# A one-row attention and MLP mix: the output weights streamed as the moving operand, the result kept as a row, other score shares, and b2 on another queue

## The chip, the cores and the metric

The kernel runs on one core of one Trainium2 chip. The metric is the device time in microseconds; shown are the median of three runs and the one execution that the profiler recorded. A core has TensorE (PE), VectorE (DVE), ScalarE (ACT), GpSimd (POOL) and SyncE (SP), each with its own instruction stream. They wait for each other by semaphores. DMAs are issued from an engine's stream; nearly all of this kernel's come from SyncE.

## The reference

One token goes through two branches, and a gate mixes them:

```python
g = sigmoid((x * gate_w).sum(-1, keepdims=True))
q = (x @ wq) as 32 heads of 128;  k, v: caches of 32 heads x 4096 x 128, bf16
o = softmax(q k^T * 128**-0.5) v            # per head, one query row
a = o.reshape(1, 1, 4096) @ wo              # wo: 4096 x 512
b = relu(x @ w1 + b1)**2 @ w2 + b2          # 512 -> 1376 -> 512
return g * a + (1 - g) * b                  # 512 values
```

The caches are 67.1 MB together, the four weight matrices some 11.2 MB. Each is read once.

## The kernel before

**Tiles.** Four heads make one tile, so there are eight tiles (`NQ`). A partition holds 128 consecutive positions of one head (32 partitions per head, `NB` = 128 "blocks" of 128 values). A K tile and a V tile are 4 MB each. K tiles go round three buffers `Kt`, V tiles round two buffers `Vt`; the last two V tiles go into `Kt` (`VT`). The weights wq lie in `Vt` slot 1, wo in `Vt` slot 0, and w1 and w2 in `Kt` slot 2, where K tile 2 (the third) goes later.

**Scores in three shares.** Of the 128 blocks of a tile, 4 times 17 (`GP`, `GB`) are multiplied on GpSimd (L301) and summed on VectorE (`psums`, L662). Two times 14 (`XP`, `XH`) are multiplied and summed on VectorE (`prods` L649, `sums` L657). The last 32 are transposed on TensorE (L424) in four pieces of eight, copied by ScalarE (L330), multiplied by q on TensorE (`scores`, L438) and copied beside the others (`score_copy`, L336). VectorE takes the maximum (L669), TensorE and VectorE bring it to one value per head (`max_rows` L448, L673, `max_cols` L452), ScalarE takes the exponentials (L347). `pv` (L469) multiplies them with V in four column groups of TensorE; `pv_copy` (L353) and `extract` (L478) collect each head's row in `O`.

**Order of the loads.** SyncE issues wq, K0, w1, w2 in three pieces, eight small pieces of w2 (L272, behind a wait for a memset of their place), K1 and V0. `load_k(2)` waits for the MLP's last matmul (`s_ml`, set after L528), since the MLP weights lie in its slot. Then the V and K tiles alternate, each behind a wait for its buffer, then wo in five pieces (L283) and the output (L286). The small vectors x, gate_w, b1 and b2 are issued by ScalarE (L308 to L311).

**Order at the start.** TensorE turns x into columns, then transposes b2 (L393), projects q in eight groups of four matmuls (L409), with a transpose of each finished group between them (`q_columns`, L400), and goes on to tile 0 (transposes, scores), the MLP's hidden row (L499, L502), its columns (L510), and the second matrix (L528). VectorE computes the gate (L620 to L624), then b2 times 1 - g (`b2g`, L627), then copies the odd groups of q (`qb`, L637), then starts on the tiles. ScalarE copies the even groups (L322). `q_columns` of a group waits for its copy, and a projection into a PSUM tile `T` waits for the copy of the group three before.

**End.** After the last `extract`, VectorE divides (L711), `regroup` (L540) and a copy (L713) put the attention row into 128 partitions x 32 columns, `o2`. `attn_out` (L549) runs through the 32 row groups of wo: per group four matmuls with a 128 x 128 piece of wo as the weights and one column of o2 as the moving operand. They add into `acc`, four columns that already hold the MLP's output (`mlp_cols`, L534). VectorE adds b2g (L716), TensorE transposes to four rows (L593), VectorE copies (L718), SyncE stores.

Of the kernel before, what the change touches and what calls it, by code (L numbers as in the profile page):

```python
# [5 lines left out]
def bass_gated_mix__gqa_block_cached__dense_activation_squared_relu__decode_kernel(  # L6
# [43 lines left out]
    GB = 17  # L50
    XP = 2
    XH = 14
    XB = GP * GB + XP * XH
    YB = NB - XB
    TC = 8
    NC = YB // TC
# [8 lines left out]
    BIG = 3.0e38  # L65
    TS = [0, 8, 16, 24, 30, 32]
    NW = len(TS) - 1

# [10 lines left out]
    with ctx:  # L79
# [18 lines left out]
        pr = sb("pr", [128, XH, 128], fp32)  # L98
        pg = sb("pg", [128, 2, GB, 128], fp32)
# [12 lines left out]
        b2r = sb("b2r", [4, 128], bf16)  # L112
# [4 lines left out]
        fin4 = sb("fin4", [4, 128], bf16)  # L117
# [23 lines left out]
        b2g = sb("b2g", [128, 4], fp32)  # L141
        fin = sb("fin", [128, 4], bf16)

        T = [pb(f"T{i}", [128, 512], fp32) for i in range(NT)]
# [11 lines left out]
        B2 = pS[:, 400:402].bitcast(bf16)  # L156
        H = pX[:, 160:160 + FN + TX]
        HX = pX[:, 224:224 + TX]
        acc = pX[:, 256:260]
# [8 lines left out]
        S = pS[:, 0:4 * YB].rearrange("p (b h) -> p b h", h=4)  # L168
# [7 lines left out]
        s_b2 = sem("s_b2")  # L176
        s_oc = sem("s_oc")
        s_o2 = sem("s_o2")
        s_fT = sem("s_fT")
        s_f4 = sem("s_f4")  # L180
# [42 lines left out]
        s_mc = sem("s_mc")  # L223
        s_hv = sem("s_hv")
# [6 lines left out]
        with nc.Block() as block:  # L231

            @block.sync
            def _(eng):
                def load_k(i):
                    if i >= NK:
                        eng.wait_ge(s_t, NC * (i - NK + 1))
                        eng.wait_ge(s_mu, XP * (i - NK + 1))
                        eng.wait_ge(s_pm, GP * (i - NK + 1))
                    if i == 2:  # L240
                        eng.wait_ge(s_ml, 1)
                    eng.dma_start(Kt[:, i % NK, :], k_p[i * 128:(i + 1) * 128, :]).then_inc(s_k[i % NK], 16)

                def load_v(i):
                    if i == 1:
                        eng.wait_ge(s_qr, NQ)
                        eng.wait_ge(s_h, 2)
                    if i < NQ - 2:
                        if i >= NV:
                            eng.wait_ge(s_pv, i - NV + 1)  # L250
                        eng.dma_start(VT(i), v_p[i * 128:(i + 1) * 128, :]).then_inc(s_v[i % NV], 16)
                        return
                    eng.wait_ge(s_t, NC * i)
                    eng.wait_ge(s_mu, XP * i)
                    eng.wait_ge(s_pm, GP * i)
                    if i == NQ - 2:
                        eng.dma_start(VT(i), v_p[i * 128:(i + 1) * 128, :]).then_inc(s_vl[0], 16)
                    else:
                        for u in range(2):
                            eng.dma_start(VT(i)[:, u * 8192:(u + 1) * 8192],  # L260
                                          v_p[i * 128:(i + 1) * 128, u * 8192:(u + 1) * 8192])\
                               .then_inc(s_vl[1 + u], 16)
# [6 lines left out]
                eng.wait_ge(s_wm, 1)  # L269
# [15 lines left out]
                eng.wait_ge(s_f4, 1)  # L285
                eng.dma_start(out[0, 0, :].rearrange("(j p) -> j p", p=128), fin4[:, :]).then_inc(s_out, 16)  # L286

            @block.gpsimd
            def _(eng):
# [4 lines left out]
                for i in range(NQ):  # L294
                    eng.wait_ge(s_k[i % NK], 16 * (i // NK + 1))
                    eng.wait_ge(s_qd if i % 2 else s_qb, 4 * (i // 2 + 1))
                    for k in range(GP):
                        n = GP * i + k
                        if n >= 2:
                            eng.wait_ge(s_ps, n - 1)  # L300
                        eng.tensor_tensor(pg[:, n % 2, :, :], Kt[:, i % NK, k * GB * 128:(k + 1) * GB * 128]  # L301
                                          .rearrange("p (b d) -> p b d", b=GB),
                                          qb[:, i:i + 1, :].broadcast_to([128, GB, 128]), ALU.mult)\
                           .then_inc(s_pm, 1)

            @block.scalar
            def _(eng):
# [3 lines left out]
                eng.dma_start(b2r[:, :], B_b2.rearrange("(j p) -> j p", p=128)).then_inc(s_b, 16)  # L311
# [20 lines left out]
                def score_copy(i):  # L332
                    eng.wait_ge(s_sc, NC * (i + 1))
                    for h in range(4):
                        a, b = HP * h, HP * h + HP
                        eng.activation(Sb[a:b, i % NS, XB:NB], S[a:b, :, h], ACT.Copy).then_inc(s_cp, 1)  # L336
# [18 lines left out]
                for i in range(NQ + 1):  # L355
                    if i == NQ:
                        pv_copy(NQ - 3)
                        pv_copy(NQ - 2)
                    if i < NQ:
                        for c in range(NC):  # L360
                            evac(i * NC + c)
                            if c == 1 and i >= 3:
                                pv_copy(i - 3)
                        score_copy(i)
                        if i == 0:
                            eng.wait_ge(s_h, 1)
                            for u, a in enumerate(range(0, F, 512)):
                                b = min(a + 512, F)
                                eng.activation(hrow[:, a:b], T[u][0:1, 0:b - a], ACT.Copy).then_inc(s_hw, 1)
# [4 lines left out]
                    if i >= 1:  # L374
                        neg_max(i - 1)
                        exps(i - 1)
                pv_copy(NQ - 1)

            @block.tensor
            def _(eng):  # L380
# [11 lines left out]
                eng.wait_ge(s_b, 32)  # L392
                eng.transpose(B2, b2r[:, :], ident[0:4, 0:4]).then_inc(s_b2, 1)  # L393
# [22 lines left out]
                def transposes(n):  # L416
                    i, c = n // NC, n % NC
# [4 lines left out]
                    for y in range(TC):  # L422
                        w = XB + c * TC + y
# [4 lines left out]
                def scores(n):  # L428
                    i, c = n // NC, n % NC
# [26 lines left out]
                def pv(i, a, b):  # L456
# [8 lines left out]
                    if a == NG // 2 and i == NQ - 1:  # L465
# [29 lines left out]
                def mlp_h():  # L495
                    eng.wait_ge(s_w1, 16)
                    parts = [(u, a, min(a + 512, F)) for u, a in enumerate(range(0, F, 512))]
# [8 lines left out]
                def mlp_c():  # L506
                    eng.wait_ge(s_hw, 3)
# [23 lines left out]
                def mlp_cols():  # L531
                    eng.wait_ge(s_mc, 1)
                    for j in range(4):
                        eng.matmul(acc[:, j:j + 1], pvf[0:112, j * 128:j * 128 + 128], pick[0:112, 0, 28:29],  # L534
                                   start=(j == 0), stop=False, skip_group_check=True)
# [9 lines left out]
                def attn_out(c):  # L545
                    eng.wait_ge(s_wo[c], 16)
                    for t in range(TS[c], TS[c + 1]):
                        for j in range(4):
                            mm = eng.matmul(acc[:, j:j + 1], wo_sb[:, t, j * 128:(j + 1) * 128],  # L549
                                            o2[:, t:t + 1], start=False, stop=(t == 31),  # L550
                                            skip_group_check=True)
                    if c == NW - 1:
                        mm.then_inc(s_acc, 1)

                for i in range(NQ):
                    for c in range(NC):
                        transposes(i * NC + c)
                        if c >= 2:
                            scores(i * NC + c - 2)
                    scores(i * NC + NC - 2)  # L560
                    scores(i * NC + NC - 1)
# [15 lines left out]
                    if i >= 2:  # L577
                        pv(i - 2, NG // 2, NG)
                extract(NQ - 3)
                pv(NQ - 2, 0, NG // 2)  # L580
                pv(NQ - 2, NG // 2, NG)
                max_rows(NQ - 1)
                max_cols(NQ - 1)
                extract(NQ - 2)
                den()
                pv(NQ - 1, 0, NG // 2)
                pv(NQ - 1, NG // 2, NG)
                extract(NQ - 1)
                regroup()
                for c in range(NW):  # L590
                    attn_out(c)
                eng.wait_ge(s_fin, 1)
                eng.transpose(T[2][0:4, 0:64].bitcast(bf16), fin[:, :], ident[:, :]).then_inc(s_fT, 1)  # L593

            @block.vector
            def _(eng):
                eng.memset(WX, 0.0).then_inc(s_wm, 1)
# [28 lines left out]
                eng.wait_ge(s_b2, 1)  # L626
                eng.tensor_scalar(b2g[:, :], B2, omg[:, 0:1], None, ALU.mult)\  # L627
# [13 lines left out]
                def prods(i, u):  # L641
# [4 lines left out]
                    if n >= 1:  # L646
                        eng.wait_ge(s_sd, n)
                    a = GP * GB + u * XH
                    eng.tensor_tensor(pr[:, :, :], Kt[:, i % NK, a * 128:(a + XH) * 128]  # L649
                                      .rearrange("p (b d) -> p b d", b=XH),  # L650
                                      PQ[:, i % 4:i % 4 + 1, :].broadcast_to([128, XH, 128]), ALU.mult)\
                       .then_inc(s_mu, 1)

                def sums(i, u):
                    eng.wait_ge(s_mu, XP * i + u + 1)
                    a = GP * GB + u * XH
                    eng.tensor_reduce(Sb[:, i % NS, a:a + XH], pr[:, :, :], AX.X, ALU.add).then_inc(s_sd, 1)  # L657

                def psums(i, k):
                    n = GP * i + k  # L660
                    eng.wait_ge(s_pm, n + 1)
                    eng.tensor_reduce(Sb[:, i % NS, k * GB:(k + 1) * GB], pg[:, n % 2, :, :], AX.X, ALU.add)\  # L662
# [53 lines left out]
                eng.tensor_tensor(fin[:, :], acc[:, 0:4], b2g[:, :], ALU.add).then_inc(s_fin, 1)  # L716
                eng.wait_ge(s_fT, 1)
                eng.tensor_copy(fin4[:, :], T[2][0:4, 0:64].bitcast(bf16)).then_inc(s_f4, 1)  # L718
# [29 lines left out]
```

## Time and profile before

| | |
|---|---|
| median of three runs | 190.68 us (190.45 to 191.6) |
| the profiled execution | 191.37 us, of which the span from first to last instruction is 189.9 us |
| DVE busy | 154.5 us, 81% of the span |
| POOL busy | 137.8 us, 73% |
| PE busy | 108.5 us, 57% |
| ACT busy | 69.4 us, 37% |
| moved by DMA | 78.47 MB, 413 GB/s over the span |

Times in the profile's timeline count from the start of the span. A row there gives start and length in us, engine, line, operation, what is written from what, and in brackets the idle time ahead of it and what ended it. In the list of groups a row gives total busy time and the mean of one instruction in ns. In the list of waits a row gives total us, number and the longest. DMA rows end with the us from issue to landing.

### The profile page before, as it was taken

What the parts mean: (1) busy time and instruction counts of PE and PEld (TensorE: products, weight loads), DVE (VectorE), ACT (ScalarE), POOL (GpSimd) and SP (SyncE); (2) the same over time, 40 slices, a digit from 0 to 9 for tenths busy, and PEclk for the clock granted to TensorE, in tenths of its full rate; (3) what the DMA queues carried; (4) which work ended last, traced back from release to release, by engine and by line L of the source; (5) the groups of instructions that cost most, each with busy time, mean ns of one, the idle gap of its engine ahead of it and who ended that gap; (6) DMA issues with size and microseconds to landing.
All of it is one profiled execution on the core that took longest, in us unless ns stands there. A gap on an engine that the chain in (4) does not pass through costs nothing. (4 is left out here: it accounts for less than half of the span.)

```text
span 189.9 us, 2665 instructions
## 1 busy us (share of the span) xinstructions
PE 108.5 (57%) x1092; PEld 67.4 (35%) x1092; DVE 154.5 (81%) x134; ACT 69.4 (37%) x170; POOL 137.8 (73%) x38
## 2 busy tenths in 40 slices
PE   1129867658213549408922881468076818685866
PEld 0113243318213516405712461327041814343245
DVE  6112479799999999999999999999999999994010
ACT  2103455208151807800960294049105730613210
POOL 1000299948799899989998999899989989970000
PEclk9999999556755855855575575586755555566555
DMA  6999999999999999999999999999999999999990
GB/s 221 443 442 442 399 470 404 428 421 421 440 437 435 428 442 438 435 414 421 421 431 442 435 435 425 421 442 442 425 421 421 435 442 442 390 425 418 419 389 30
DMA packets 3840, 78.47 MB, mean 413 GB/s; under 512 B 483, under 2 KB 589, under 8 KB 886
## 3 DMA queue, kind: packets, MB, share of 16 engines
q1 hardware_dynamic: 3816, 78.32, 96.7%
q8 instruction: 8, 0.13, 0.3%
q14 instruction: 2, 0.02, 0.0%
q10 hardware_dynamic: 14, 0.01, 0.0%
HBM read 78.32 MB, written 0.00 MB: 412 GB/s over the span
## 5 line engine op out<-in xcount | busy, mean ns | idle before, releaser
L301 POOL TENSOR_TENSOR pg<-Kt,qb 128x2176 f32<-128x2176 bf16 x32 | 137.1, 4316 | 31.1 <-DMA Kt<-in_A_k_cache_dram 21.1
L662 DVE TENSOR_REDUCE Sb<-pg 128x17 f32<-128x2176 f32 x32 | 76.9, 2404 | 0.0
L330 ACT ACTIVATE kT<-T 128x1024 bf16<-128x1024 bf16 x32 | 30.8, 1030 | 7.0 <-PE T L424 6.7
L649 DVE TENSOR_TENSOR pr<-Kt,pQ 128x1792 f32<-128x1792 bf16 x16 | 32.2, 2011 | 1.0
L657 DVE TENSOR_REDUCE Sb<-pr 128x14 f32<-128x1792 f32 x16 | 32.0, 2003 | 0.0
L424 PE MATMUL T<-ident,Kt 128*128 128x128 bf16 x256 | 26.2, 285 | 8.3 <-DMA Kt<-in_A_k_cache_dram 8.3
L424 PEld LDWEIGHTS T<-ident,Kt 128*128 128x128 bf16 x256 | 22.9, 133 | 12.8 <-DMA Kt<-in_A_k_cache_dram 9.8
L469 PE MATMUL pO<-Vt,E 128*16 128x512 bf16 x192 | 25.1, 604 | 0.0
L340 ACT ACTIVATE nM<-pM 128x4 f32<-128x4 f32 x8 | 1.4, 173 | 62.0 <-PE pM L452 62.0
L448 PE MATMUL pM<-identf,mp 128*1 128x128 f32 x8 | 2.9, 360 | 31.2 <-DVE mp L669 31.2
L347 ACT ACTIVATE E<-Sb,nM 32x128 bf16<-32x128 f32 x32 | 18.8, 586 | 1.0
L438 PE MATMUL pS<-qc,kT 128*128 128x4 bf16 x256 | 11.7, 168 | 9.3 <-ACT kT L330 9.0
L478 PE MATMUL pX<-pvf,pick 112*32 112x128 f32 x64 | 15.3, 421 | 2.3 <-ACT pvf L353 2.3
L438 PEld LDWEIGHTS pS<-qc,kT 128*128 128x128 bf16 x256 | 9.9, 102 | 11.4 <-ACT kT L330 11.3
L478 PEld LDWEIGHTS pX<-pvf,pick 112*32 112x32 f32 x64 | 9.9, 168 | 7.0 <-ACT pvf L353 4.1
L448 PEld LDWEIGHTS pM<-identf,mp 128*1 128x1 f32 x8 | 0.6, 80 | 32.3 <-DVE mp L669 32.3
L637 DVE CAST qb<-T 32x128 bf16<-32x128 f32 x16 | 4.6, 287 | 7.8 <-PE T L409 7.4
L409 PE MATMUL T<-Vt,kT 128*128 128x512 bf16 x32 | 10.7, 485 | 0.1
L452 PE MATMUL pM<-gm,onesf 1*128 1x4 f32 x16 | 4.5, 348 | 9.4 <-DVE gm L673 9.4
L469 PEld LDWEIGHTS pO<-Vt,E 128*16 128x16 bf16 x192 | 7.1, 110 | 6.7 <-issue 5.0
L452 PEld LDWEIGHTS pM<-gm,onesf 1*128 1x128 f32 x16 | 3.8, 292 | 15.4 <-DVE gm L673 15.4
L347 ACT ACTIVATION_READ_ACCUMULATOR E<-Sb,nM 32x1 f32 x32 | 8.2, 257 | 0.0
(80 smaller groups left out, 74.8 us busy)
## 6 DMA issues: line engine op xcount, KB each, us to landing
Kt<-in_A_k_cache_dram SPq DMA_DIRECT2D x8, 4096.0 KB, 28.1
Vt<-in_A_v_cache_dram SPq DMA_DIRECT2D x6, 4096.0 KB, 28.9
Vt<-in_A_wq_dram SPq DMA_DIRECT2D x1, 4096.0 KB, 12.2
Kt<-in_A_v_cache_dram SPq DMA_DIRECT2D x1, 4096.0 KB, 33.1
Kt<-in_A_v_cache_dram SPq DMA_DIRECT2D x2, 2048.0 KB, 22.2
Vt<-in_A_wo_dram SPq DMA_DIRECT2D x3, 1024.0 KB, 28.5
Kt<-in_B_w_dram SPq DMA_DIRECT2D x1, 1376.0 KB, 24.1
Kt<-in_B_w_dram SPq DMA_DIRECT2D x1, 1152.0 KB
```

What stands on the lines that cost most here:

```text
L301: eng.tensor_tensor(pg[:, n % 2, :, :], Kt[:, i % NK, k * GB * 128:(k + 1) * GB * 128] .rearrange("p (b d) -> p b d", b=GB), qb[:, i:i + 1 ...
L330: eng.activation(kT[:, n % NR, :], T[n % NT][:, :].bitcast(bf16), ACT.Copy).then_inc(s_ev, 1)
L347: eng.activation(E[a:b, j % NE, :, h], Sb[a:b, j % NS, :], ACT.Exp, bias=nM[a:b, 4 * j + h:4 * j + h + 1], scale=SCALE, accum_out=RS[a:b, ...
L409: mm = eng.matmul(T[j % NT][:, :], xb[:, t, :], wq_sb[:, t, j * 512:(j + 1) * 512], start=(t == 0), stop=(t == 3))
L424: mm = eng.transpose(T[n % NT][:, :].bitcast(bf16)[:, y * 128:(y + 1) * 128], Kt[:, i % NK, w * 128:(w + 1) * 128], ident[:, :])
L438: mm = eng.matmul(S[:, c * TC + y, :], kT[:, n % NR, y * 128:(y + 1) * 128], qc[:, 4 * i:4 * i + 4], start=True, stop=True)
L452: eng.matmul(MB[:, 4 * i:4 * i + 4], onesf[:, :], gm[:, 4 * i:4 * i + 4], start=True, stop=True) .then_inc(s_mb, 1)
L469: mm = eng.matmul(pO[r:r + 16, :], E[:, i % NE, 4 * y:4 * y + 4, :], VT(i)[:, y * 512:(y + 1) * 512], start=(y < 4), stop=(y >= NG - 4))
L478: mm = eng.matmul(O, pick[0:112, b, 28 - 4 * i:60 - 4 * i], pvf[:, b * 128:(b + 1) * 128], start=False, stop=(i == NQ - 1 and b == 3), ski ...
L649: eng.tensor_tensor(pr[:, :, :], Kt[:, i % NK, a * 128:(a + XH) * 128] .rearrange("p (b d) -> p b d", b=XH), PQ[:, i % 4:i % 4 + 1, :].bro ...
L657: eng.tensor_reduce(Sb[:, i % NS, a:a + XH], pr[:, :, :], AX.X, ALU.add).then_inc(s_sd, 1)
L662: eng.tensor_reduce(Sb[:, i % NS, k * GB:(k + 1) * GB], pg[:, n % 2, :, :], AX.X, ALU.add)\
```

## The change

- `attn_rows` replaces `attn_out`: a column of o2 is the weights, and wo streams past as the moving operand. The first 20 of the 32 row groups are taken with all 512 columns, four row groups side by side in `pO`; the other 12 with 128 columns in each of four column groups, into rows 0, 32, 64 and 96 of `acc`. ScalarE copies `pO` once more (`s_ww`, `s_wc`) and `wide_rows` adds its four rows into `acc` with four fp32 matmuls, between the third and the fourth wo piece.
- The result is a row: `acc` is 128 x 128 with four rows in use, VectorE adds `b2g` (now 128 x 128) into `b2w`, and SyncE stores from there. The transpose and the copy at the end go. `mlp_cols` writes rows too.
- b2 is no longer loaded by ScalarE and transposed. SyncE loads it into four rows of `b2w` after w2's first three pieces, behind a wait for two memsets; VectorE's `b2g` waits for that load (`s_bb`).
- Tiles 3 to 7 have five pieces of eight blocks on TensorE (40 blocks), 16 blocks in a GpSimd piece, 12 in a VectorE piece; tiles 0 to 2 stay at 32, 17 and 14.
- V's last tile is loaded and used as 96 and 32 blocks (`VG` = 24 groups of four) instead of 64 and 64.
- At the end, `max_rows` and `max_cols` of the last tile go ahead of `pv` of the last but one; ScalarE's copy of that `pv` goes behind the last exponentials.
- The MLP's hidden row is copied by one ScalarE instruction instead of three.

```diff
-    GB = 17
-    XH = 14
-    NC = YB // TC
+    NC = [4 if i < 3 else 5 for i in range(NQ)]
+    CB = [sum(NC[:i]) for i in range(NQ + 1)]
+    GB = [17 if n == 4 else 16 for n in NC]
+    XH = [14 if n == 4 else 12 for n in NC]
...
+    WW = 20
+    VG = 24
...
-        acc = pX[:, 256:260]
+        acc = pX[:, 0:128]
...
@@ sync
-                        for u in range(2):
-                            eng.dma_start(VT(i)[:, u * 8192:(u + 1) * 8192],
-                                          v_p[i * 128:(i + 1) * 128, u * 8192:(u + 1) * 8192])\
-                               .then_inc(s_vl[1 + u], 16)
+                        for u, a, b in ((1, 0, VG * 512), (2, VG * 512, NG * 512)):
+                            eng.dma_start(VT(i)[:, a:b], v_p[i * 128:(i + 1) * 128, a:b]).then_inc(s_vl[u], 16)
...
                 eng.dma_start(w2b[96:FR, :], B_w2[F0 + 96:F1, :]).then_inc(s_w2, 16)
-                eng.wait_ge(s_wm, 1)
+                eng.wait_ge(s_wm, 2)
+                eng.dma_start(b2w[0:128:32, :], B_b2.rearrange("(j p) -> j p", p=128)).then_inc(s_bb, 16)
                 for r in range(4):
...
-                eng.wait_ge(s_f4, 1)
-                eng.dma_start(out[0, 0, :].rearrange("(j p) -> j p", p=128), fin4[:, :]).then_inc(s_out, 16)
+                eng.wait_ge(s_fin, 1)
+                eng.dma_start(out[0, 0, :].rearrange("(j p) -> j p", p=128), b2w[0:128:32, :]).then_inc(s_out, 16)
@@ scalar
-                eng.dma_start(b2r[:, :], B_b2.rearrange("(j p) -> j p", p=128)).then_inc(s_b, 16)
...
-                            for u, a in enumerate(range(0, F, 512)):
-                                b = min(a + 512, F)
-                                eng.activation(hrow[:, a:b], T[u][0:1, 0:b - a], ACT.Copy).then_inc(s_hw, 1)
+                            eng.activation(hrow, TT[0:1, 0:F], ACT.Copy).then_inc(s_hw, 1)
...
+                pv_copy(NQ - 2)
                 pv_copy(NQ - 1)
+                eng.wait_ge(s_ww, 1)
+                eng.activation(pvf[:, :], pO[0:112, :], ACT.Copy).then_inc(s_wc, 1)
@@ tensor
-                eng.wait_ge(s_b, 32)
-                eng.transpose(B2, b2r[:, :], ident[0:4, 0:4]).then_inc(s_b2, 1)
...
-                        eng.matmul(acc[:, j:j + 1], pvf[0:112, j * 128:j * 128 + 128], pick[0:112, 0, 28:29],
-                                   start=(j == 0), stop=False, skip_group_check=True)
+                        eng.matmul(acc[32 * j:32 * j + 32, :], pick[0:112, 0, 28:60], pvf[0:112, j * 128:j * 128 + 128],
+                                   start=True, stop=False, skip_group_check=True)
...
-                def attn_out(c):
+                def attn_rows(c):
                     eng.wait_ge(s_wo[c], 16)
                     for t in range(TS[c], TS[c + 1]):
+                        r = 32 * (t % 4)
+                        if t < WW:
+                            mm = eng.matmul(pO[r:r + 1, :], o2[:, t:t + 1], wo_sb[:, t, :], start=(t < 4),
+                                            stop=(t >= WW - 4), skip_group_check=True)
+                            if t == WW - 1:
+                                mm.then_inc(s_ww, 1)
+                            continue
                         for j in range(4):
-                            mm = eng.matmul(acc[:, j:j + 1], wo_sb[:, t, j * 128:(j + 1) * 128],
-                                            o2[:, t:t + 1], start=False, stop=(t == 31),
-                                            skip_group_check=True)
+                            mm = eng.matmul(acc[32 * j:32 * j + 1, :], o2[:, t:t + 1],
+                                            wo_sb[:, t, j * 128:(j + 1) * 128], start=False,
+                                            stop=(t == 31), skip_group_check=True)
...
+                def wide_rows():
+                    eng.wait_ge(s_wc, 1)
+                    for j in range(4):
+                        eng.matmul(acc[32 * j:32 * j + 1, :], pick[0:112, 0, 28:29], pvf[:, j * 128:(j + 1) * 128],
+                                   start=False, stop=False, skip_group_check=True)
...
+                max_rows(NQ - 1)
                 extract(NQ - 3)
-                pv(NQ - 2, 0, NG // 2)
-                pv(NQ - 2, NG // 2, NG)
-                max_rows(NQ - 1)
                 max_cols(NQ - 1)
+                pv(NQ - 2, 0, NG)
                 extract(NQ - 2)
                 den()
-                pv(NQ - 1, 0, NG // 2)
-                pv(NQ - 1, NG // 2, NG)
+                pv(NQ - 1, 0, VG)
+                pv(NQ - 1, VG, NG)
                 extract(NQ - 1)
                 regroup()
                 for c in range(NW):
-                    attn_out(c)
-                eng.wait_ge(s_fin, 1)
-                eng.transpose(T[2][0:4, 0:64].bitcast(bf16), fin[:, :], ident[:, :]).then_inc(s_fT, 1)
+                    if c == NW - 2:
+                        wide_rows()
+                    attn_rows(c)
@@ vector
+                eng.memset(b2w[:, :], 0.0).then_inc(s_wm, 1)
...
                 eng.wait_ge(s_g, 3)
-                eng.wait_ge(s_b2, 1)
-                eng.tensor_scalar(b2g[:, :], B2, omg[:, 0:1], None, ALU.mult)\
+                eng.wait_ge(s_bb, 16)
+                eng.tensor_scalar(b2g[:, :], b2w[:, :], omg[:, 0:1], None, ALU.mult)\
                    .then_inc(s_g, 1)
...
-                eng.tensor_tensor(fin[:, :], acc[:, 0:4], b2g[:, :], ALU.add).then_inc(s_fin, 1)
-                eng.wait_ge(s_fT, 1)
-                eng.tensor_copy(fin4[:, :], T[2][0:4, 0:64].bitcast(bf16)).then_inc(s_f4, 1)
+                eng.tensor_tensor(b2w[:, :], acc, b2g[:, :], ALU.add).then_inc(s_fin, 1)
```

## The prediction

> **What bounds the kernel now.** I read the page first: busy shares, the forty slices, the queues.
>
> ```profile
> PE 108.5 (57%) x1092; PEld 67.4 (35%) x1092; DVE 154.5 (81%) x134; ACT 69.4 (37%) x170; POOL 137.8 (73%) x38
> ...
> DMA  6999999999999999999999999999999999999990
> ...
> q1 hardware_dynamic: 3816, 78.32, 96.7%
> ```
>
> No engine is as full as SyncE's queue q1: 78.32 MB, busy in every slice but the first and the last. Every microsecond in which this queue runs dry moves the end. DVE comes second; it sets the end of the softmax.
>
> Then the end, in the timeline from 184 us, and the landing of the five wo pieces (source view of L283, its last line):
>
> ```profile
> 184.31 3.58 PE L549 MATMUL pX<-o,Vt 128*128 128x1 bf16 x128 [0.29 <-DVE o L713]
> 187.92 0.16 DVE L716 TENSOR_TENSOR fin<-pX,b2g 128x4 bf16<-128x4 f32 x1 [3.67 <-PE pX L549]
> 188.14 0.27 PE L593 MATMUL T<-ident,fin 128*4 128x128 bf16 x1 [0.26 <-DVE fin L716]
> 188.45 0.21 DVE L718 COPY fin<-T 4x128 bf16<-4x128 bf16 x1 [0.36 <-PE T L593]
> ```
> ```profile
> L283 SPq DMA_DIRECT2D Vt<-in_A_wo_dram x5: 422/432/433, 152.6 to 154.4; - x5
> ...
> DMA to landing us min/median/max: 26.5/30.5/32.0
> ```
>
> The last wo piece, issued at 154.4, lands 32.0 us later, about 186.6; the chain, bound by DVE's last maximum at 172.4, ends its matmuls at 187.90. The two are only 1.3 us apart. So a faster softmax can win little: the DMA's end is close behind.
>
> Last the start, by the timeline, the queue's own waits and the DMA issues between 3 and 20 us:
>
> ```profile
> 13.04 0.22 DVE L627 TENSOR_SCALAR b2g<-pS,omg 128x4 f32<-128x4 bf16 x1 [2.88 <-PE pS L393]
> 16.63 1.24 DVE L637 CAST qb<-T 32x128 bf16<-32x128 f32 x4 [3.36 <-PE T L409]
> 17.92 0.10 PEld L400 LDWEIGHTS pX<-ident,qb 128*128 128x128 bf16 x1 [0.43 <-DVE qb L637]
> 25.86 2.02 DVE L649 TENSOR_TENSOR pr<-Kt,pQ 128x1792 f32<-128x1792 bf16 x1
> ...
> 42.53 0.80 SPq L242 DMA_DIRECT2D Kt<-in_A_k_cache_dram  x2
> ```
> ```profile
> SPq L242 <- PE pO L528: 32.2, 1, 32.2
> ```
> ```profile
> Kt<-in_A_k_cache_dram SPq DMA_DIRECT2D x1, 4096.0 KB, 30.8
> Vt<-in_A_v_cache_dram SPq DMA_DIRECT2D x1, 4096.0 KB, 40.1
> ```
>
> The third K tile (K2) shares its buffer with the MLP weights, so SyncE waits 32.2 us for the MLP's last matmul and issues K2 at 42.53. V0, issued at 9.85, lands 40.1 later, at 50.0; K2 is then next and lands at 59.9 (17.4 after its issue). The queue therefore has about 6 us in hand: K2 can be issued up to about 48.7 before the engines run dry (50.0 less the 1.3 us that wq's first bytes took from its issue).
>
> **Step 1: b2 comes late.** Before, b2r is issued at 1.82 on ScalarE's queue and TensorE reads it at 12.75, while waiting for wq anyway (13.02). Now b2w stands on SyncE's queue behind wq, K0, w1 and w2. These land in order, K1 40.2, V0 50.0, K2 59.9, K3 69.5, V1 79.3. w1 (issued 1.63, 24.1 to landing) lands at 25.8; w2a's 1.18 MB at 423 GB/s (window 20 to 30) adds 2.8, the two rest pieces 0.2: b2w lands at about 28.8. Bounds: 12.6, as b2r had it, if small loads pass large ones; 30 if it lands with the small loads behind it. I take 28.8, since five landings in a row kept the order.
>
> The row for landings is in order. The Trainium skill, "DMA: Bandwidth & Descriptors", section "Queues, rings and completion order", says that each DMA engine takes descriptors in ring order but that a DMA on few engines may complete before an earlier one on all sixteen. By it b2w's four rows could be ahead by as much as the engines differ, but not by a whole 4 MB load; this speaks against rival 1 below, and no run here shows b2w itself.
>
> **Step 2: who is queued behind it.** DVE does b2g in program order ahead of everything else that it does for q and the tiles. It waits until 28.8, takes about 0.28 (nearest row: 128x128 CAST into pQ, 275 ns), and only then copies qb of group 1 (L637): at 29.2 instead of 16.63, 12.6 later. TensorE stands at the transpose of that qb (17.92, released by DVE) and projects no further. The rest, L637 of group 1 to the first product of tile 0 (L649), took 9.2 us. With the same length the product begins at 38.4. The first eight projection matmuls took 3.57 us, 446 ns each, the last four 1.03, 258 each; at the slow rate throughout, five groups of four through the DVE and ACT copies come to 10.8, and L649 begins at 40.0. I take 39.3, +13.4 (12.5 to 14.3).
>
> This bears on a rule of the Trainium skill, "TensorE: Matmul & The Clock Gate", section "Part 1: The HAM clock gate": after an idle window of some 3.4 us the array starts at half clock again. By it the slow end, +14.3, would hold for most of the chain.
>
> **Step 3: the queue runs dry.** Tile 0's transposes, mlp_h, mlp_c, mlp_x and mlp_out follow on TensorE in the same order, and their copies in DVE's order; all move by 13.4. The hidden-row copy as one ACTIVATE of 1376 elements instead of three (1.41 together) saves about 0.1: 512 against 352 elements differ by 0.13 us, so one takes 1.3. K2 is issued at 42.53 + 13.4 = 55.9. wq, which found an empty queue, took 12.2 from issue to landing; a load in the stream takes 9.7. K2 lands between 55.9 + 12.2 = 68.1 and 55.9 + 1.3 + 9.7 = 66.9, against 59.9: 7.0 to 8.2 later. I take 7.7. Everything behind it moves by as much: V7's last piece (151.7 + 24.9 = 176.7) to 184.4, the last of wo from 186.6 to 194.3. No second hole: K4 was issued at 61.67, V2 at 73.98, each 10 us or more before its turn, and DVE's lateness then only shrinks.
>
> **Step 4: the shares.** In tiles 3 to 7 a POOL product and its reduction have 16 blocks, not 17, DVE's own products 12, not 14.
>
> ```profile
> L662 DVE TENSOR_REDUCE Sb<-pg 128x17 f32<-128x2176 f32 x32 | 76.9, 2404 | 0.0
> ...
> L649 DVE TENSOR_TENSOR pr<-Kt,pQ 128x1792 f32<-128x1792 bf16 x16 | 32.2, 2011 | 1.0
> L657 DVE TENSOR_REDUCE Sb<-pr 128x14 f32<-128x1792 f32 x16 | 32.0, 2003 | 0.0
> ```
>
> By size: 4 x 141 + 2 x 287 + 2 x 286 = 1.71 us a tile, 8.5 in five. POOL (4316 ns, 4 a tile) falls to 16.2 a tile beside DVE's 16.3, so it does not stop the gain. TensorE's eight more transposes and scores and ACT's one more copy (1030 ns) lie in idle time (PE 57%, ACT 37%). The last maximum comes at 172.4 + 13.4 - 8.5 = 177.3, the last exponential (4.3 later) at 181.6, before V7's last piece at 184.4. So this gain covers the lateness of DVE and is otherwise hidden behind the DMA; without it the maximum would come at 185.8 and be the bound.
>
> **Step 5: the end.** From V7's last piece: 8 matmuls 0.9 (L469: 32 in 3.50), copy 0.65, extraction 1.95, oT, regroup, o2 1.05: 188.9. The wo pieces of 2.45 us each end at 189.5, 191.9, 193.7, 194.3 after the first at 187.0. Wide rows: by L469 (109 ns each, four column groups side by side) 20 take 2.2; 48 narrow ones at a quarter 1.3; together 3.5, what L549's 128 took (3.58), so the form itself wins nothing. The third piece at 191.9, 4 wide 0.45, ACT's copy 0.65, then wide_rows: four fp32 matmuls, between 0.5 side by side and 1.93 in line (L478: 8 passes in 1.91). I take 0.6, as for L469, so they end at 193.7, when the fourth piece lands. Its 24 narrow take 0.7 (194.4), the last 8 0.25: 194.7. The sum over 128 elements takes 0.30 instead of 0.16; transpose and copy (0.55) fall away. From the last copy's end (188.66) to the span's end (189.9) it is 1.24. Span: 194.7 + 0.1 + 0.35 + 1.24 = 196.4, **+6.5**. The smaller moves (extract and max_cols order, mlp_cols with 128 columns, some 1 us beside DVE) lie in TensorE's idle time.
>
> The profiled execution took 191.37 for a span of 189.9; the median is 190.68. Added to the median: **197.2**.
>
> **Rivals.** (1) b2 does not hold DVE: it lands early, or anywhere before about 22, since DVE's first qb copy may be 6 us late before K2 is late; that is the point from which it decides. Then wo ends at 186.6 as before, the matmuls at 187.0, the span at 188.7: 1.2 less, 189.5. For it: nothing but that b2 is 1 KB; against: the order of landings. This is the case on the other side, faster by 0.6%, and with a better end by up to 1.2%. Chance 0.08. (2) The wait is there, but part of the MLP catches up (full clock for mlp_h, DVE's wait of 1.19 for the hidden column used): K2 at 53 to 54.5, 193 to 195.5. Chance 0.12. (3) The end is serial: wide_rows in line costs 1.3 more, the last 32 narrow ones in line (109 each, a quarter of four times 109, instead of 27) up to 2.6 more: 198.5 to 201. The MLP's first 15 matmuls at the slow rate add up to 1.8 (459 columns on average, 400 ns each, 6.0, against 4.2). Chance 0.18. (4) DVE does not gain by size and stays the bound: maximum at 185.8, then the 15.5 us that it took from there to the last matmul: 202.5 and more. Chance 0.02. My forecast, 195.5 to 198.5, has 0.60.
>
> The range 193.5 to 200.5 leaves out (1), (4) and the far ends. Faster by over 1% 0.03, within 1% 0.06, slower 0.91; 1% is about what a measurement of this kernel can tell from no change.
>
> **What would show it.** After: DVE's b2g waits some 18 us, released by the DMA of b2w near 28.8 (step 1); L637 first near 29.2 and L649 near 39.3 (2); SyncE's wait for L528 of about 45, and slices near 50 to 57 with idle DMA (3); tile periods of 16.3 from tile 3 (4); TensorE waiting for wo in its last 6 us, and fp32 rows side by side (5). I am wrong if b2w lands before 22, if K2 is issued before 49, or if the stream catches up a gap, which at 99% share it has no room for.

## The result, and the profile after

The changed kernel takes 202.01 us (median of five runs, 201.16 to 203.19), the kernel before, run beside it, 191.45. The ratio is 1.057, with a 95% interval of 1.051 to 1.062. The forecast was slower, 197.2 us in a range of 193.5 to 200.5. Direction and cause were right, the size was too small, and the time lies above the range. The profiled execution took 201.16 us for a span of 199.7: 9.8 more than the 189.9 of before, where 6.5 were forecast.

The page after, its slices, its data queue and the queue for instruction fetches:

```profile
PE 105.5 (53%) x1118; PEld 62.4 (31%) x1118; DVE 147.1 (74%) x134; ACT 74.6 (37%) x174; POOL 132.9 (67%) x38
...
DMA  7999899995049999999999999999999999999991
...
q1 hardware_dynamic: 3824, 78.32, 92.2%
q8 instruction: 9, 0.15, 0.3%
```

The bytes are the same, but q1 is busy for 92.2% of the span instead of 96.7%, and there is a hole in the eleventh slice and the ones beside it. It lies between 48 and 58 us, as the answer for these stretches shows (stretch, its length, busy time of each engine with the number of instructions, granted clock, DMA share, GB/s):

```profile
46.00:48.00 2.00, 2.00 (x6) 0.39 (x5) 2.00 (x2) 0.60 (x4) 2.00 (x1) 0.50 0.80 336
48.00:50.00 2.00, 2.00 (x8) 0.76 (x7) 2.00 (x2) 0.00 (x0) 2.00 (x2) 0.65 0.06 16
50.00:56.00 6.00, 3.31 (x28) 1.75 (x26) 4.25 (x9) 1.48 (x2) 3.90 (x1) 0.73 0.00 0
56.00:58.00 2.00, 2.00 (x18) 1.41 (x17) 2.00 (x2) 0.85 (x2) 1.31 (x1) 0.50 0.69 180
```

What led to it, in the timeline of the changed kernel and in the queue's own waits:

```profile
29.48 2.04 DVE L645 TENSOR_SCALAR b2g<-b2w,omg 128x128 f32<-128x128 bf16 x1 [19.25 <-DMA b2w<-in_B_b_dram]
31.44 1.24 DVE L655 CAST qb<-T 32x128 bf16<-32x128 f32 x4
...
40.90 2.02 DVE L668 TENSOR_TENSOR pr<-Kt,pQ 128x1792 f32<-128x1792 bf16 x1
...
56.79 0.80 SPq L249 DMA_DIRECT2D Kt<-in_A_k_cache_dram  x2
```
```profile
SPq L249 <- PE pO L533: 45.8, 1, 45.8
```

VectorE stands 19.25 us for b2. Its first q copy starts at 31.44 instead of 16.63, its first product of tile 0 at 40.90 instead of 25.86, and SyncE issues K2 at 56.79 instead of 42.53.

The end, in the timeline:

```profile
196.63 1.02 PE L561 MATMUL pX<-Vt,o 128*1 128x128 bf16 x32 [0.38 <-DMA Vt<-in_A_wo_dram]
197.70 0.29 DVE L737 TENSOR_TENSOR b2w<-pX,b2g 128x128 bf16<-128x128 f32 x1 [5.85 <-PE pX L561]
198.02 0.60 SPq L292 DMA_DIRECT2D out_dram<-b2w  x1
```

TensorE now waits for wo. In the trace's landing records the last wo piece lands at 197.21 (before: 186.47), and 2.49 us later the span ends. Before, the chain behind the softmax set the end; now the stream does.

### The profile page after: what moved, and what is told of

Read it like the earlier page. It is cut to its first block, busy times and chain, and to the rows that moved or that the text cites. A ratio compares the mean times of both kernels' runs of the same rounds, so it can differ in the third digit from the quotient of the medians.

```text
span 199.7 us, 2722 instructions
## 1 busy us (share of the span) xinstructions
PE 105.5 (53%) x1118; PEld 62.4 (31%) x1118; DVE 147.1 (74%) x134; ACT 74.6 (37%) x174; POOL 132.9 (67%) x38
## 3 DMA queue, kind: packets, MB, share of 16 engines
q1 hardware_dynamic: 3824, 78.32, 92.2%
## 5 line engine op out<-in xcount | busy, mean ns | idle before, releaser
L308 POOL TENSOR_TENSOR pg<-Kt,qb 128x2048 f32<-128x2048 bf16 (+1 forms) x32 | 132.2, 4163 | 42.8 <-DMA Kt<-in_A_k_cache_dram 21.4
L683 DVE TENSOR_REDUCE Sb<-pg 128x16 f32<-128x2048 f32 (+1 forms) x32 | 74.3, 2322 | 0.1
L336 ACT ACTIVATE kT<-T 128x1024 bf16<-128x1024 bf16 x37 | 35.3, 1034 | 5.5 <-PE T L428 5.2
L668 DVE TENSOR_TENSOR pr<-Kt,pQ 128x1536 f32<-128x1536 bf16 (+1 forms) x16 | 29.5, 1844 | 1.0
L677 DVE TENSOR_REDUCE Sb<-pr 128x12 f32<-128x1536 f32 (+1 forms) x16 | 29.4, 1837 | 0.0
L473 PE MATMUL pO<-Vt,E 128*16 128x512 bf16 x192 | 23.2, 577 | 1.6 <-issue 1.6
L645 DVE TENSOR_SCALAR b2g<-b2w,omg 128x128 f32<-128x128 bf16 x1 | 2.0, 2039 | 19.3 <-DMA b2w<-in_B_b_dram 19.3
L328 ACT ACTIVATE qb<-T 32x128 bf16<-32x128 f32 x16 | 4.3, 268 | 25.8 <-PE T L413 25.5
L482 PE MATMUL pX<-pvf,pick 112*32 112x128 f32 x64 | 13.1, 374 | 1.4 <-ACT pvf L359 1.4
L482 PEld LDWEIGHTS pX<-pvf,pick 112*32 112x32 f32 x64 | 8.7, 148 | 5.2 <-ACT pvf L359 2.8
L404 PE MATMUL pX<-ident,qb 128*128 128x128 bf16 x8 | 2.1, 258 | 15.5 <-DVE qb L655 15.0
```

The lines of the kernel that those rows point to most:

```text
L308: eng.tensor_tensor(pg[:, n % 2, 0:g, :], Kt[:, i % NK, k * g * 128:(k + 1) * g * 128] .rearrange("p (b d) -> p b d", b=g), qb[:, i:i + 1, ...
L328: eng.activation(qb[a:b, j, :], T[j % NT][a:b, h * 128:(h + 1) * 128], ACT.Copy)\
L336: eng.activation(kT[:, n % NR, :], T[n % NT][:, :].bitcast(bf16), ACT.Copy).then_inc(s_ev, 1)
L473: mm = eng.matmul(pO[r:r + 16, :], E[:, i % NE, 4 * y:4 * y + 4, :], VT(i)[:, y * 512:(y + 1) * 512], start=(y < 4), stop=(y >= NG - 4))
L482: mm = eng.matmul(O, pick[0:112, b, 28 - 4 * i:60 - 4 * i], pvf[:, b * 128:(b + 1) * 128], start=False, stop=(i == NQ - 1 and b == 3), ski ...
L668: eng.tensor_tensor(pr[:, 0:x, :], Kt[:, i % NK, a * 128:(a + x) * 128] .rearrange("p (b d) -> p b d", b=x), PQ[:, i % 4:i % 4 + 1, :].bro ...
```

## The experiments

My theory: b2g waits for a load behind four large ones, VectorE holds up the q projection and the MLP, K2's issue is late, the queue runs dry, and the stream never makes that up. The rivals were that the new end or the shares cost the time, that 1 KB among large loads disturbs the stream, and, for the 2.04 us of b2g, that its form is slow by itself.

**b2 from ScalarE's queue.**

```diff
-                eng.dma_start(b2w[0:128:32, :], B_b2.rearrange("(j p) -> j p", p=128)).then_inc(s_bb, 16)   # sync
+                eng.wait_ge(s_wm, 1)                                                                         # scalar, behind b1
+                eng.dma_start(b2w[0:128:32, :], B_b2.rearrange("(j p) -> j p", p=128)).then_inc(s_bb, 16)
```

> The changed kernel with one edit: b2's load into the four rows of b2w is issued by ScalarE behind b1, as b2r was before, not by SyncE behind K0, w1 and w2. Theory (b2g waits for b2 and holds VectorE, the MLP, K2 and so the DMA queue): b2w lands near 13, b2g takes about 0.3 us, K2 is issued near 42.5, the last wo piece lands near 186.7 as before the change, and with the 2.25 us that the changed kernel needs from that landing to its end the span is 189.0, 0.9 less than before; ratio 0.990 to 0.998. Rival (the new output form, the shares or the order at the end cost the time): the span stays above 195.

Measured: 191.11 us against 190.85, ratio 1.0014 (0.9996 to 1.0032), span 189.4. The timeline:

```profile
12.80 0.28 DVE L646 TENSOR_SCALAR b2g<-b2w,omg 128x128 f32<-128x128 bf16 x1 [2.63 <-DMA b2w<-in_B_b_dram]
...
43.07 0.80 SPq L249 DMA_DIRECT2D Kt<-in_A_k_cache_dram  x2
```

The whole loss is gone with this one edit. The rest of the change is then worth nothing measurable: I expected a ratio of 0.990 to 0.998. The last wo piece lands at 186.89, so the stream sets the end here too (the chain of the end has 36 us of that DMA in it), and the 6 us by which VectorE's last maximum now comes earlier (166.31 instead of 172.40) are hidden behind it.

**b2g at the end of VectorE's program, the load where the change has it.**

```diff
-                            eng.wait_ge(s_g, 4)                # tensor, ahead of the first scores
+                            eng.wait_ge(s_g, 3)
...
                 eng.wait_ge(s_g, 3)                            # vector
-                eng.wait_ge(s_bb, 16)
-                eng.tensor_scalar(b2g[:, :], b2w[:, :], omg[:, 0:1], None, ALU.mult).then_inc(s_g, 1)
...
+                eng.wait_ge(s_bb, 16)
+                eng.tensor_scalar(b2g[:, :], b2w[:, :], omg[:, 0:1], None, ALU.mult).then_inc(s_g, 1)
                 eng.wait_ge(s_den, 1)
```

> The changed kernel with b2's load where the change put it, on SyncE's queue, but b2g (with its wait for the load) moved in VectorE's order from ahead of q to behind the last tile; the first scores wait for the gate alone. Theory: what costs is the wait at that place in VectorE's order, not the place of the load; span 189.0 as with the early load, K2 issued near 42.5, ratio 0.990 to 0.998. Rival (1 KB on few DMA engines among the large loads disturbs the stream itself): the last wo piece still lands later than 190.

Measured: 191.15 us, ratio 1.001 (0.999 to 1.003), span 189.4, K2 issued at 42.89, wo's last landing 186.94. So the load's place is harmless; the wait's place in VectorE's order is what costs.

**GpSimd's first product behind b2g.**

```diff
+                eng.wait_ge(s_g, 4)          # gpsimd, ahead of the tiles
                 for i in range(NQ):
```

> The changed kernel, with GpSimd's first product waiting until b2g is done. In the changed kernel b2g took 2.04 us where 0.28 was forecast, and ended as GpSimd's second product ended (31.44). Theory (VectorE's b2g stands still while GpSimd's product runs): b2g takes about 0.3 us, K2 is issued 1.7 us earlier, near 55.0, the span is 198.0 against 199.7. Rival (the form 128x128 bf16 to f32 with a scalar per partition costs 2 us by itself): b2g stays at 2.0 us and the span at 199.7 or more.

Measured: 200.61 us, ratio 1.051 (1.048 to 1.054), span 198.8.

```profile
29.89 0.29 DVE L646 TENSOR_SCALAR b2g<-b2w,omg 128x128 f32<-128x128 bf16 x1 [19.54 <-DMA b2w<-in_B_b_dram]
30.26 8.55 POOL L309 TENSOR_TENSOR pg<-Kt,qb 128x2176 f32<-128x2176 bf16 x2 [28.80 <-DVE b2g L646]
...
56.02 0.80 SPq L249 DMA_DIRECT2D Kt<-in_A_k_cache_dram  x2
```

b2g takes 0.29 us when no product runs beside it, so the 2.04 were not its form's. The span fell by 0.9, not 1.7: b2 itself landed 0.4 later in this run, and from the first q copy to the first product it took 0.6 longer.

**b2 right behind K0.**

```diff
                 load_k(0)
+                eng.wait_ge(s_wm, 1)
+                eng.dma_start(b2w[0:128:32, :], B_b2.rearrange("(j p) -> j p", p=128)).then_inc(s_bb, 16)
...
                 eng.wait_ge(s_wm, 2)
-                eng.dma_start(b2w[0:128:32, :], B_b2.rearrange("(j p) -> j p", p=128)).then_inc(s_bb, 16)
```

> The changed kernel with b2's load on SyncE's queue right behind K0, ahead of w1 and w2: it lands near 23.0. A dose between none and full. If b2g waits for the end of a GpSimd product (the first runs from 22.9 to 27.2), VectorE goes on at 27.2, K2 is issued near 52.6, and the span is 195.2, since the engines run dry at 48.4 and the first packets of an empty queue take 0.85 longer. If b2g takes 2 us by itself: K2 near 50.5, span 193.1. If it takes 0.3: K2 near 48.7, span near 191. If, as my prediction had it, the queue has work until 50.0, each of these is 1.6 less.

Measured: 197.68 us, ratio 1.033 (1.030 to 1.037), span 195.9. The timeline:

```profile
22.83 8.54 POOL L309 TENSOR_TENSOR pg<-Kt,qb 128x2176 f32<-128x2176 bf16 x2 [21.36 <-DMA Kt<-in_A_k_cache_dram]
22.98 4.22 DVE L646 TENSOR_SCALAR b2g<-b2w,omg 128x128 f32<-128x128 bf16 x1 [12.54 <-DMA b2w<-in_B_b_dram]
...
52.93 0.80 SPq L249 DMA_DIRECT2D Kt<-in_A_k_cache_dram  x2
```

The first of the three cases, to 0.7 us. b2g starts 0.15 after GpSimd's first product and ends at 27.20, half way through the two products of 8.54, that is where the first of them ends (22.83 + 4.27 = 27.10). An instruction of 0.28 us took 4.22.

**The kernel before, with the late wait alone.**

```diff
                 eng.wait_ge(s_wm, 1)                                    # sync
+                eng.dma_start(b2w[0:128:32, :], B_b2.rearrange("(j p) -> j p", p=128)).then_inc(s_bb, 16)
...
                 eng.wait_ge(s_b2, 1)                                    # vector, ahead of b2g
+                eng.wait_ge(s_bb, 16)
```

> The kernel before with one thing added: SyncE loads the same 1 KB of b2 into a tile that is not used otherwise, at the place where the change puts it, and VectorE waits for it ahead of b2g; all else is as before, old shares, old end. Theory: this wait alone makes the loss. VectorE copies its first q group near 29.9, K2 is issued near 55.8, first landing of K2's parts 11.9 us later against 58.1 before, so the stream is 9.5 late and wo ends near 196.2; VectorE keeps its old shares, so its last maximum comes at 172.4 + 13.4 = 185.8 and, with the 17.5 us from there to the end, the span is 203.3, more than the changed kernel's 199.7: the new shares save 3.6 of the loss. Rival (the shares play no part): 189.9 + 9.5 = 199.4.

Measured: 204.48 us, ratio 1.071 (1.066 to 1.075), span 202.8 (expected 203.3). The timeline:

```profile
29.78 0.22 DVE L631 TENSOR_SCALAR b2g<-pS,omg 128x4 f32<-128x4 bf16 x1 [19.41 <-DMA b2w<-in_B_b_dram]
...
55.41 0.80 SPq L244 DMA_DIRECT2D Kt<-in_A_k_cache_dram  x2
...
185.28 0.29 DVE L673 TENSOR_REDUCE mp<-Sb 128x1 f32<-128x128 f32 x1
```

The wait, put into the old kernel, makes the loss by itself. wo lands at 195.99, yet the span ends at 202.8: without the new shares VectorE is the bound again, and the changed kernel's 199.7 is 3.1 better. So the shares did their part: from the first product to the last maximum VectorE takes 138.0 us in the changed kernel, 145.8 here. They paid for VectorE's lateness and had nothing left for the stream's. The 3.1 are not the shares' alone, since this run has the old end too and a short b2g.

**No stall, old shares.**

```diff
-    NC = [4 if i < 3 else 5 for i in range(NQ)]
+    NC = [4 for i in range(NQ)]
```

(on top of b2 from ScalarE's queue)

> The kernel with b2 on ScalarE's queue (no stall), and in all eight tiles the old shares: 32 blocks on TensorE, 17 and 14 blocks a piece elsewhere. Theory: without the stall the shares still move VectorE's last maximum, from 166.3 to 172.9, but only because the end becomes bound by it: exponentials end 5.8 later at 178.7, pv, copy, extraction and regrouping end near 186.0, the output rows with their copy near 190.5, span 192.5, ratio 1.010 to 1.018. Rival (the DMA end at 187.1 covers all of it): span 189.4 to 190, ratio 1.00.

Measured: 192.08 us, ratio 1.007 (1.004 to 1.010), span 189.8: between the two. The chain of the end, in order of time, has at its start (start us, us, what):

```profile
172.81 0.30 DVE mp L691
173.10 0.04 issue
173.15 0.37 PE pM L453
173.52 1.85 PE pX L483 x8
175.37 0.53 PE pM L457 x2
```

VectorE's maximum came at 172.81, as forecast (172.9), and the new order at the end puts the extraction of another tile (1.85 us) between its two halves, which the old order did not. But from there to the last matmul it took 15.0 us, where I had 17.6: TensorE ran this end at its fast rate (20 wide rows in 1.28, forecast 2.2; granted clock 1.00 from 178 to 188, where the kernel before had 0.50). So the chain ends only 1.0 after wo's last landing (186.80). This execution was the fastest of ten; the others' spans go up to 192.3, and why is not shown, since no trace of them was kept. Without the stall the shares are worth about 1 us (191.11 against 192.08, each beside its own runs of before).

**V1 ahead of K2.**

```diff
                 load_v(0)
+                load_v(1)
                 load_k(2)
...
-                    if i >= 1:
+                    if i >= 2:
                         load_v(i)
```

> The changed kernel, with b2 late as the change has it, but V1 issued ahead of K2 on SyncE. V1 waits for the MLP's hidden columns (53.3 in the changed kernel), K2 for the MLP's end (56.8). Theory (all of the loss is the time in which the queue has nothing to do): the hole ends 3.4 us earlier, the span is 196.3, ratio 1.027 to 1.036, although K2 itself lands later, near 77. Rival (the loss is that K2 and the tiles behind it come late): no gain or a loss, 199.7 or more.

Measured: 198.44 us, ratio 1.039 (1.036 to 1.042), span 196.9. V1 was issued at 54.21 (from the first q copy to the first product it took 0.7 longer here), K2 at 57.56, and K2 landed at 77.2, 6.5 later than in the changed kernel; still the kernel is 2.8 us of span faster. What counts is when the queue has something to do, not K2.

Put together, the first load behind the hole was issued at 52.93, 54.21, 56.02 and 56.79, and the spans are 195.9, 196.9, 198.8 and 199.7: 6.5, 7.5, 9.4 and 10.3 above the 189.4 without a stall. Issue less loss is 46.4, 46.7, 46.6 and 46.5. **From 52.9 to 56.8 us every microsecond of a later issue is one of the result, and the line through the four runs comes to no loss at 46.5 us.** That point is the line carried back; no run issued the load that follows V0 between 43.1 and 52.9.

**The rest of w2 in two loads.** An attempt at a version faster than both kernels, on top of b2 from ScalarE's queue, since the landings of a load spread over the engines by up to 2 us and the stream is the bound.

```diff
                 eng.wait_ge(s_wm, 2)                            # sync
-                for r in range(4):
-                    for p, q in ((0, 0), (32, 20)):
-                        eng.dma_start(WX[p + r:p + 20:4, :], w2_x[q + r:q + 20:4, :]).then_inc(s_w2, 16)
+                for p, q in ((0, 0), (32, 20)):
+                    eng.dma_start(WX[p:p + 20, :], w2_x[q:q + 20, :]).then_inc(s_w2, 16)
...
-                    eng.wait_ge(s_w2, 16 * 11)                  # tensor, ahead of the second matrix
+                    eng.wait_ge(s_w2, 16 * 5)
```

> The kernel with b2 on ScalarE's queue (no stall), and the last 120 rows of w2 loaded by two DMAs of 20 partitions instead of eight of 5. In that kernel the DMA stream is the bound, and in the traces the landings of one tile are spread over the engines by about 2 us from K1 on, right behind these eight loads. Theory: eight loads on few engines put those behind the others; with two loads the spread of K1's landing falls from 1.8 to about 1 us, the last wo piece lands near 186.5 instead of 187.1, the time falls by 0.3 to 0.6 us, ratio to the kernel before 0.996 to 1.000. Rival: the spread comes from elsewhere (the instruction fetches on q8), time and spread as they were, ratio 1.001.

Measured: 191.58 us, ratio 1.0035 (1.0017 to 1.0054). The landings of K1 spread over 1.7 us (38.99 to 40.65) against 1.8 (38.68 to 40.47), and wo's last is at 187.27. The theory of the eight loads is half right. With them, five of K1's sixteen landings come 1.0 to 1.3 us behind the first and one 1.8; with two loads fifteen lie within 0.8 us, and one still comes at 1.7. The trace has a cause for that one: an instruction fetch (queue 8, 16 KB) at 32.6 for 1.10 us, behind which one packet of the stream took 1.68 instead of 1.21; the later fetches up to 152.6 each have such a packet behind them too (1.59 to 1.88). This is read from the trace alone, as no run moved a fetch. No version that I ran beats the kernel before.

## Why the prediction was right and where it was not

- **Step 1, b2 comes late: right.** b2g starts at 29.48, forecast 28.8. The order of landings held, 1 KB included.
- **Step 2, who is queued behind it: right, one term mis-sized.** b2g cost 2.04 us instead of 0.28, because GpSimd's second product ran from about 27.2 to 31.4 (third and fourth experiment). I had priced it by the CAST into pQ, which writes PSUM and is not held up (0.29 beside a product, at 51.34). The trace of before had the better row, which I did not read: three 128x9 instructions that took 1.81 together beside a product, and 0.51 in the changed kernel, where none was running any more.

```profile
38.12 1.81 DVE L683 SCALAR_TENSOR_TENSOR hs<-hr,omg 128x9 bf16<-128x9 f32 x3
```
```profile
53.67 0.51 DVE L704 SCALAR_TENSOR_TENSOR hs<-hr,omg 128x9 bf16<-128x9 f32 x3
```

  From the first q copy to the first product it took 9.46, forecast 10.1; the slow first matmuls were there (1.91, 1.58, then 1.03 for four; granted clock 0.50 from 32.7 to 34.6 and 1.00 from 36.1), so the chosen middle was a little high. The Trainium skill, "TensorE: Matmul & The Clock Gate", section "Part 1: The HAM clock gate", has the array start at half clock after an idle window. This trace agrees, but the slow rate held for some 3 of the 9.46 us, not for most of the chain. L668 came at 40.90, forecast 39.3.
- **Step 3, the queue runs dry: right in kind, and the step that failed.** K2 was issued at 56.79, forecast 55.9 (the MLP took 0.8 less than before: the three small instructions, not held up, gave 1.3, and the hidden row's matmuls took 0.6 more). The term that failed is the way of a load through an empty queue. I took 11.7 us from K2's issue to its landing, between 11.0 and 12.2; it took 13.9, and K2 landed at 70.67 instead of 67.6. Fourteen of its sixteen landings came 11.6 to 12.1 after the issue, inside my bounds. The other two came at 13.0 and 13.9: by the times of the packets, two engines each had an instruction fetch in between (0.96 us on queue 8 at 65.18, 0.31 on queue 14 at 67.28), and behind it a packet of K2 took 1.68 and 1.75 instead of 1.21. So the hole did level the engines, nearly as far as in wq's row (landings within 0.4), but the fetches drew them apart again within the same load. Of wo's last piece, the last landing comes 10.7 later than before, the first 10.4.
  Told as a reserve, the line through the runs gives 46.5, where I had 48.7 and the sum used 48.2. I had counted from V0's landing, 50.0, as the time at which the engines have nothing left. It is the landing of the last of sixteen: V0's landings in the kernel before begin at 48.16, and in the stretch from 48 to 50 of the changed kernel the DMA share is 0.06. The first packets behind the hole took 1.4 to 2.3 us each, where one in the stream takes 1.21. Three figures were off as well, by less: wq's first bytes came 1.0 after its issue, not 1.3; 154.4 + 32.0 is 186.4, not 186.6; and the slow end of step 2, 40.0, is 14.1 after 25.86, not 14.3. wo ended at 197.21, forecast 194.3.
- **Step 4, the shares: right.** Maxima follow each other at 16.4 us from tile 3 on (forecast 16.3; the last, of tile 7, after 14.5) and at 18.0 and 17.7 ahead of it. The last comes at 178.88, forecast 177.3, 1.6 later, as L668 was. Without the shares VectorE would be the bound: 185.28 in the fifth experiment, 185.8 by the sum.
- **Step 5, the end: right.** From wo's last landing to the end of the span 2.49, forecast 2.1: SyncE's store took 0.60, where the old one took 0.30. The four fp32 matmuls of `wide_rows` took 0.40, so the serial end of the third rival is out; of the 1.8 that it put on the MLP's first matmuls, 0.6 came.
- **The rivals.** The first (b2 does not hold VectorE) did not happen; made to happen, it is not 1.2 us faster but equal: wo's last landing was 0.4 later than before, the end 0.4 longer than the sum, and the profiled 189.9 of before lies high among its spans (189.0 to 190.4 beside the first experiment). The second (the MLP catches up) gave 0.8, by luck: from the three small instructions, not from the causes that it named. The fourth is refuted by the tile period.

The span is 3.3 above the forecast: 0.9 by K2's later issue, 2.2 by its longer way to the last landing, 0.4 by the end, less 0.2 between K2's landing and wo's. The median is another 1.5 further off. I had added 6.5 to 190.68, the median of three runs, where the profiled execution of before took 191.37 (0.7), and the changed kernel's profiled execution was the fastest of its five, 0.85 below the median.

## What to carry to other kernels

A small load that an engine waits for early must not stand behind large ones in the queue, and where it must, the wait belongs as late in the engine's order as its result is needed: the second experiment moved one instruction and won 10 us of span. In a kernel bound by its DMA stream, work out first how late the next issue may come, with the first engine's end and not the last landing, because beyond that each microsecond counts in full (measured here from 52.9 us on), and below it a faster engine wins nothing.

## What the runs showed of the hardware that I had not expected

- A VectorE instruction of 0.28 us stood still until GpSimd's running product ended: 2.04, 1.97 and 4.22 us (changed kernel, seventh and fourth experiment), by where in the product it started, and 0.29 with none beside it (third). With its source in PSUM (fifth experiment, 128x4) it took 0.22 while a product ran, and the reductions were not held up (L683 2.41 with and without a product beside it). The Trainium skill, "SBUF — State Buffer", section "Who interferes with whom", has the rule: VectorE's second pair of SBUF ports is GpSimd's too and is locked for a whole instruction, and a scalar multiply or one with two SBUF sources may need it. These runs agree; the rule would have given the missing 1.8 us of step 2.
- An empty queue costs more than the time it is empty: 1.0 us from issue to the first packet, and 1.4 to 2.3 instead of 1.21 for each engine's first.
- By the times of the packets, instruction fetches run on the same DMA engines as the stream. In the changed kernel the nine of queue 8 (16 KB) took 0.96 to 1.10 us each, and the seven that met a load's 32 KB packets have one of 1.68 to 1.76 instead of 1.21 behind them. One engine falls back by some 1.5 us each time, an estimate from these two, and the landings do not draw together again: those of wo's last piece lie 2.2 us apart (195.03 to 197.21).
- fp32 matmuls with one column of weights in four column groups run side by side: `wide_rows`' eight passes took 0.40, against 1.06 for the eight of an `extract` in the same kernel (L482).
